# Attention and a gated Mish MLP on one core: the PSUM layout of the scores, the order of the engines and the spread of 1/den are changed together

## The chip, the core and the metric

The kernel runs on one core of one Trainium2 chip. The metric is the device time in microseconds (us) of one launch. PE is the engine of the matmuls, ACT the engine of the activations (here the exponential), DVE the vector engine, SP the engine that issues most DMAs. PSUM, which the matmuls write into, is used as eight banks of 128 x 512 f32. The granted clock is the share of its full clock that PE was allowed.

## The reference

```python
a = softmax(q k^T * Dh**-0.5) v @ wo       # S = 2048, D = 640, H = 32 heads, Dh = 20
h = x @ w1 + b1                            # F = 1536
b = (h * tanh(softplus(h))) @ w2           # Mish MLP
g = sigmoid((x * gate_w).sum(-1))
return g * a + (1 - g) * b                 # bf16 inputs
```

## The kernel before

The work of the attention is 2048 **blocks**: 128 keys x 512 queries of one head. Four heads share the row strips of PE, and 64 blocks make a **group** (one chunk of 512 queries, four heads), of which there are 32. Each block needs a score matmul, an exponential and a PV matmul. Four blocks (the four heads) form one **quad** of PV, whose matmuls run side by side in the column strips of PE.

The exponentials are the largest job. ACT does most of them, 2 or 3 blocks in one instruction. 232 of the 2048 blocks go to DVE. It turns the scores into bits of an exponential with a first pass out of PSUM (`dA`, one per block, 0.69 us), and then works on pairs of blocks in a chain of five operations that leaves three bf16 terms (`dN`, `dA`, `dB`) whose sum is the exponential. PV of such a block therefore takes three rounds where others take one.

PSUM before: score tiles alternate between 3 and 2 banks (5 banks), one bank is the accumulator of PV (`acc`), and 2 banks serve the projections (x transposed, k, q, v, the MLP and `wo`) and also the scores of the DVE blocks, which are computed up to 20 blocks ahead.

```python
WIDTHS = (3, 2); LEAD = 20
banks = [psum.tile([P, QC], F32, tag=f"bank{i}", name=f"bank{i}") for i in range(2)]
epool = ctx.enter_context(tc.tile_pool(name="epool", bufs=3))

def emit_D(n):                              # scores of a DVE block: a projection bank
    d = banks[ubank[0] ^ 1]
    bank_free[ubank[0] ^ 1] = now[0] + 1
    scores(d[:, :], blocks[n])
    nc.vector.tensor_scalar(out=A[:, i, :], in0=d[:, :], scalar1=exp_c, scalar2=0.0,
                            op0=ALU.add, op1=ALU.max)            # first pass
    # [cut: every second block queues the chain of five operations]

for t, ns in enumerate(tiles):              # one turn per score tile
    w = WIDTHS[t % 2]
    E = epool.tile([P, w, QC], BF16, tag=f"E{t % 2}", bufs=3 - t % 2, name="E")
    nc.scalar.activation(E[:, 0:nw, :], sp.pop(t)[:, 0:nw, :], ACT.Exp, scale=escale)
    emit_S(t + 2)                           # the next scores into the same tile
    # [cut: emit_D at most every second turn; two operations of the DVE chain]
    used += pv_quads(min(tiles[t + 1][0], n_end), t)             # PV of blocks before tile t+1
    credit -= pump(min(credit, max(room, 300.0)), 1)             # projections, fixed budget
```

At the end of a group, `acc` is copied to `accS`, its row of denominators goes through four small DMAs to `den`, DVE takes the reciprocal `rec`, four more small DMAs of 2 KB bring it to one row per strip, a shuffle on DVE spreads it over the strip, and a multiply writes `oT`.

The softmax here doesn't subtract the row's maximum and nothing guards it: scores larger than these inputs give would overflow.

## Time and profile before

| kernel before | |
|---|---|
| median of the runs | 997.37 us (993.48 to 1002.19, 4 runs) |
| profiled run: span, mean granted clock | 995.7 us, 0.902 |
| ACT busy / PE busy / DVE busy | 876.3 / 874.1 / 647.8 us |
| ACT idle from 25 us to the last exponential | 21 us in slices at full clock, 58 us in slices that touch a lowered clock |

The last row comes from cutting the span into slices of 5 us. 705 us of slices had a granted clock of 1.00, and 240 us had less.

The page of the kernel before: the span, busy time by engine (share of the span, number of instructions), busy tenths of PE, ACT and the granted clock in 40 slices, and the group of the exponentials (count, then busy us and mean ns, then idle time of ACT just before them and what ended most of it).

```profile
span 995.7 us, 15399 instructions
PE 874.1 (88%) x6181; PEld 270.5 (27%) x6250; DVE 647.8 (65%) x1269; ACT 876.3 (88%) x751; POOL 19.0 (2%) x36
...
PEclk7999999998699789999967999996999996995877
...
L755 ACT ACTIVATE E<-Sp 128x1536 bf16<-128x1536 f32 x727 | 841.0, 1261 | 80.5 <-PE Sp L576 65.3
```

Here `Sp` is a score tile in PSUM, `E` the buffer in SBUF that an exponential writes, and `<-PE Sp` says that a PE instruction on `Sp` ended the wait. PE and ACT are nearly level. ACT waits mostly for scores, 65 of its 80 us. The groups by form of the same kernel give one exponential of each width:

```profile
L755 ACT ACTIVATE E<-Sp 128x1536 bf16<-128x1536 f32 x363 | 534.8, 1473 | 54.8 <-PE Sp L576 48.6 <-PE bank_73 L576 2.4 <-PE bank_74 L576 0.7
L755 ACT ACTIVATE E<-Sp 128x1024 bf16<-128x1024 f32 x363 | 381.0, 1050 | 25.6 <-PE Sp L576 16.7 <-PE bank_73 L576 6.0 <-PE bank_74 L576 1.7
```

The widths alternate, so every pair of neighbours is of two forms. The two forms add to 915.8 us and cover 841.0, so neighbours overlap by 75 us in all, 0.10 us per exponential. The Trainium skill, "ScalarE: Activation LUTs", section "What ACT_TABLE_LOAD costs", gives about 93 ns for this overlap; the trace has somewhat more here.

The windows of the kernel before (length, then busy time and count of PE, PEld, DVE, ACT, POOL, then granted clock, DMA share, GB/s). The first is a stretch with many projections. The next three stand around a Mish step, in which ACT ran something other than exponentials and PE stood 7.71 us for a score tile. The last two belong to a later low stretch.

```profile
core 0: us, PE busy (x) PEld busy (x) DVE busy (x) ACT busy (x) POOL busy (x), PEclk, DMA share, GB/s
25.00:200.00 175.00, 162.42 (x1383) 62.37 (x1403) 100.07 (x232) 161.66 (x142) 3.12 (x6) 0.99 0.02 4
...
325.00:330.00 5.00, 2.29 (x14) 0.63 (x13) 3.88 (x8) 4.97 (x4) 0.00 (x0) 0.91 0.00 0
330.00:335.00 5.00, 0.01 (x1) 0.01 (x1) 0.00 (x0) 4.97 (x5) 0.00 (x0) 0.50 0.00 0
335.00:340.00 5.00, 5.00 (x25) 1.15 (x25) 0.79 (x2) 3.90 (x4) 0.00 (x0) 0.56 0.00 0
...
900.00:905.00 5.00, 5.00 (x23) 0.90 (x22) 0.69 (x1) 2.69 (x3) 0.00 (x0) 0.50 0.00 0
905.00:910.00 5.00, 5.00 (x23) 1.16 (x22) 3.54 (x7) 4.00 (x4) 0.00 (x0) 0.50 0.00 0
```

At half clock PE is full (5.00 of 5) and ACT is not. So two things limit this kernel: ACT at full clock, PE at half clock.

### The profile page before, as it was taken

Reading aid. Unit: us, or ns where it says so; the run is one execution under the profiler, and the core shown is the slowest. Engines: PE = TensorE matmul, PEld = TensorE weight load, DVE = VectorE, ACT = ScalarE, POOL = GpSimd, SP = SyncE. Lnnn points to the kernel's source line nnn. Section 1 sums busy time; section 2 is a strip of 40 time slices with the busy share of each in tenths; the row PEclk is TensorE's granted clock in tenths of the full one; section 3 lists DMA queues with packets and bytes.
Section 4 is the critical chain, followed back from the end, with each engine's and each line's share of the span. In section 5 each row is a group of like instructions: output and inputs, shape, how many; then the busy total and the mean of one; then the engine's idle time right before and its main releaser. Section 6 shows DMA issues by size and latency. Waiting matters only on the chain.

```text
span 995.7 us, 15399 instructions
## 1 busy us (share of the span) xinstructions
PE 874.1 (88%) x6181; PEld 270.5 (27%) x6250; DVE 647.8 (65%) x1269; ACT 876.3 (88%) x751; POOL 19.0 (2%) x36
## 2 busy tenths in 40 slices
PE   5999998888898688999979998997998969889894
PEld 2433332222222122332212322221332212221221
DVE  2455646677676567777846876774777764774665
ACT  3899999899898989999988999989999997996881
POOL 6000000000000000000000000000000000000000
PEclk7999999998699789999967999996999996995877
DMA  7100000004000000000000000000000000000000
GB/s 231 16 2 2 1 2 1 1 2 140 21 2 1 1 1 2 15 8 9 2 1 1 2 15 8 8 1 1 2 1 2 1 1 8 9 15 1 2 1 27
DMA packets 22216, 14.18 MB, mean 14 GB/s; under 512 B 15968, under 2 KB 20192, under 8 KB 22144
## 3 DMA queue, kind: packets, MB, share of 16 engines
q1 hardware_dynamic: 20512, 12.16, 4.0%
q0 software_dynamic: 320, 0.82, 0.4%
q8 instruction: 49, 0.80, 0.3%
q10 hardware_dynamic: 1312, 0.20, 0.1%
q14 instruction: 23, 0.19, 0.1%
HBM read 10.04 MB, written 2.62 MB: 13 GB/s over the span
## 4 chain that ended last, share of the span: by engine, by line
PE 45%; ACT 29%; DVE 14%; issue 7%; DMA 3%; SPq 2%; DVEq 0%; ACTq 0%; another core or an unknown queue 0%
ACT E L755 26%; PE Sp L576 13%; PE acc L649 13%; PE bank_74 L366 3%; PE bank_73 L366 3%; DVE dA L600 3%; PE bank_73 L231 2%; PE bank_74 L231 2%; ACT hst L354 2%; PE bank_74 L332 2%; PE bank_74 L576 1%; PE bank_73 L332 1%; DVE dm L626 1%; DVE rrow L685 1%; DMA rrow<-rec 1%
## 5 line engine op out<-in xcount | busy, mean ns | idle before, releaser
L755 ACT ACTIVATE E<-Sp 128x1536 bf16<-128x1536 f32 x727 | 841.0, 1261 | 80.5 <-PE Sp L576 65.3
L576 PE MATMUL Sp<-qT,kT 32*128 32x512 bf16 x1816 | 310.7, 408 | 61.8 <-ACT E L755 52.3
L649 PE MATMUL acc<-E,VA 128*32 128x512 bf16 x1816 | 214.0, 416 | 6.3 <-DVE accS L666 6.0
L576 PEld LDWEIGHTS <-kT 32*128 32x128 bf16 x2048 | 82.4, 92 | 270.1 <-issue 250.0
L600 DVE TENSOR_SCALAR dA<-bank_73 128x512 int16<-128x512 f32 x116 | 79.7, 687 | 104.6 <-PE bank_73 L576 101.0
L600 DVE TENSOR_SCALAR dA<-bank_74 128x512 int16<-128x512 f32 x116 | 79.1, 682 | 72.2 <-PE bank_74 L576 71.7
L649 PEld LDWEIGHTS <-VA 128*32 128x32 bf16 x2512 | 69.4, 96 | 188.1 <-issue 174.9
L626 DVE TENSOR_TENSOR dm<-dm 128x1024 f16<-128x1024 f16 x116 | 79.9, 689 | 2.6
L628 DVE TENSOR_TENSOR dB<-dA,dm 128x1024 bf16<-128x1024 bf16 x116 | 79.4, 684 | 0.0
L576 PE MATMUL bank_74<-qT,kT 32*128 32x512 bf16 x116 | 46.2, 398 | 13.0 <-DVE hst L340 6.4
L623 DVE TENSOR_SCALAR dm<-dm 128x1024 f16<-128x1024 bf16 x116 | 49.9, 430 | 4.0
L619 DVE TENSOR_SCALAR dm<-dA 128x1024 int16<-128x1024 int16 x116 | 49.6, 427 | 4.0
L649 PE MATMUL acc<-dN,VA 128*32 128x512 bf16 x232 | 50.0, 428 | 0.1
L649 PE MATMUL acc<-dA,VA 128*32 128x512 bf16 x232 | 49.4, 423 | 0.0
L576 PE MATMUL bank_73<-qT,kT 32*128 32x512 bf16 x116 | 47.9, 413 | 1.6 <-DVE kT L240 1.6
L649 PE MATMUL acc<-dB,VA 128*32 128x512 bf16 x232 | 49.2, 421 | 0.0
L627 DVE TENSOR_SCALAR dN<-dA 128x1024 int16<-128x1024 int16 x116 | 48.8, 420 | 0.0
L366 PE MATMUL bank_74<-w_sb,hst 128*128 128x320 bf16 x204 | 47.6, 325 | 1.0 <-DVE dA L600 0.6
L366 PEld LDWEIGHTS <-hst 128*128 128x128 bf16 x384 | 28.4, 99 | 61.0 <-issue 56.5
L366 PE MATMUL bank_73<-w_sb,hst 128*128 128x320 bf16 x180 | 41.0, 324 | 1.9 <-DVE dA L600 1.7
L332 PE MATMUL bank_74<-xT,w_sb 128*128 128x512 bf16 x115 | 38.6, 391 | 4.1 <-DVE dA L600 3.7
L666 DVE COPY accS<-acc 128x512 f32<-128x512 f32 x31 | 21.4, 690 | 24.6 <-PE acc L649 24.6
(102 smaller groups left out, 610.4 us busy)
## 6 DMA issues: line engine op xcount, KB each, us to landing
w_sb<-in_B_w_dram SPq DMA_DIRECT2D x2, 1920.0 KB, 11.1
x_sb<-in_A_x_dram SPq DMA_DIRECT2D x4, 640.0 KB, 7.7
out_dram<-ot SPq DMA_DIRECT2D x16, 160.0 KB, 1.8
den<-accS SPq DMA_DIRECT2D x124, 2.0 KB, 1.7
rrow<-rec SPq DMA_DIRECT2D x124, 2.0 KB, 1.7
W_sb<-in_A_wqkv_dram SPq DMA_DIRECT2D x1, 1600.0 KB, 15.1
W_sb<-in_A_wqkv_dram SPq DMA_DIRECT2D x1, 800.0 KB, 8.2
wo_sb<-in_A_wo_dram POOLq DMA_DIRECT2D x4, 200.0 KB, 6.6
```

Of the source, the lines that this page charges most:

```text
L231: nc.tensor.matmul(cell["t"][:, :], lhsT=lhs(kt), rhs=xT[:, kt, c * QC : (c + 1) * QC], start=(kt == 0), stop=(kt == KT - 1),)
L332: nc.tensor.matmul(cell["t"][:, :], lhsT=lw["w1"][:, kt, ft * P : (ft + 1) * P], rhs=xT[:, kt, c * QC : (c + 1) * QC], start=(kt == 0), st ...
L366: nc.tensor.matmul(cell["t"][:, :], lhsT=lhs(k, jj), rhs=rhs(k)[:, cols], start=(k == k0), stop=(k == k1 - 1),)
L576: nc.tensor.matmul(dst, lhsT=kT[R * r : R * (r + 1), p, j * P : (j + 1) * P], rhs=qTs[c, p][R * r : R * (r + 1), :], start=True, stop=True ...
L600: nc.vector.tensor_scalar(out=A[:, i, :], in0=d[:, :], scalar1=exp_c, scalar2=0.0, op0=ALU.add, op1=ALU.max)
L619: lambda: ts(out=m, in0=A, scalar1=0x7F, scalar2=0x3F80, op0=ALU.bitwise_and, op1=ALU.bitwise_or,),
L623: lambda: ts(out=t, in0=mf, scalar1=exp_k, scalar2=exp_k * EXP_M, op0=ALU.mult, op1=ALU.add),
L626: lambda: tt(out=t, in0=t, in1=t, op=ALU.mult),
L627: lambda: ts(out=N, in0=A, scalar1=0x7F80, scalar2=None, op0=ALU.bitwise_and),
L628: lambda: (tt(out=B, in0=Ab, in1=t, op=ALU.mult), done_()),
L649: nc.tensor.matmul(acc[R * r : R * (r + 1), :], lhsT=VA[:, j, p, (DH + 1) * r : (DH + 1) * r + R], rhs=es[r][k], start=(j == 0 and k == 0) ...
L755: nc.scalar.activation(E[:, 0:nw, :], sp.pop(t)[:, 0:nw, :], ACT.Exp, scale=escale)
```

## The change

The intent: put each DVE block into a score tile, so that the scores of three blocks always run together in the row strips of PE; give both score tiles three banks, and pay for that with one of the two projection banks; decide the order of PE's instructions by a virtual clock that models when each engine will be ready; and replace the four DMAs and the shuffle of 1/den by a DMA to a scratch in DRAM and one DMA back that spreads each row over its 32 partitions.

The diff also changes smaller things: estimated costs of projections, the order of some units of the MLP, 10 instead of 12 buffers for `oT`, and 236 instead of 232 DVE blocks. The diff, cut to its core:

```diff
-    WIDTHS = (3, 2)
-    LEAD = 20
+    BPT = 3
+    DPOS0 = (2, 3, 10, 11)
+    DPOS = (1, 2, 6, 7, 11, 12)
-    banks = [psum.tile([P, QC], F32, tag=f"bank{i}", name=f"bank{i}") for i in range(2)]
+    bank = psum.tile([P, QC], F32, tag="bank")
-    epool = ctx.enter_context(tc.tile_pool(name="epool", bufs=3))
+    epool = ctx.enter_context(tc.tile_pool(name="epool", bufs=5))
[cut]
+    def on_dve(t):
+        g = tiles[t][-1] // 64
+        return g > 0 and t + 2 < len(tiles) and t % 16 in (DPOS0 if g < 5 else DPOS)
[cut]
     def ahead(n):
-        return tile_at[max(0, n - LEAD)] - 4
+        return tile_at[n] - 5
[cut]
     def emit_S(t):
-        w = WIDTHS[t % 2]
-        sp[t] = psum.tile([P, w, QC], F32, tag=f"S{t % 2}", name="Sp")
-        for i, n in enumerate(tiles[t]):
+        ns = tiles[t]
+        sp[t] = psum.tile([P, BPT, QC], F32, tag=f"S{t % 2}", name="Sp")
+        for i, n in enumerate(ns):
             scores(sp[t][:, i, :], blocks[n])
+        V["pe"] = max(V["pe"], s_ready(t) - 0.1) + pe_cost(0.213, "S")
+        s_done[t] = V["pe"] + 0.23
+        if on_dve(t):
+            dve_score(ns[-1], sp[t][:, BPT - 1, :], t)     # first pass from the third bank
[cut: normalise]
+            scr = scrp.tile([4, QC], F32, tag="scr", name="scr")
+            nc.sync.dma_start(scr.rearrange("r (i n) -> (r i) n", n=ND), rec)
+            v = scr[:, :]
+            nc.sync.dma_start(rr[:, :], bass.AP(v.tensor, v.offset, [[QC, 4], [0, R], [1, QC]]))
-            nc.vector.stream_shuffle(out=rr, in_=rr, mask=[0] * R)
-        later[t + 4] = part1
-        later[t + 8] = part2
+        later.append((V["dve"] + 3.0, 0.25, part1))
+        later.append((V["dve"] + 9.0, 0.69, part2))        # the multiply
[cut: the turn of tile t]
-        E = epool.tile([P, w, QC], BF16, tag=f"E{t % 2}", bufs=3 - t % 2, name="E")
+        na = len(ns) - on_dve(t)
+        E = epool.tile([P, BPT, QC], BF16, tag="E", name="E")
+        nc.scalar.activation(E[:, 0:na, :], sp.pop(t)[:, 0:na, :], ACT.Exp, scale=escale)
+        begin = max(V["act"], s_done[t])
+        V["act"] = begin + 0.05 + 0.427 * na
+        credit = min(credit + min(rate(t), 2600.0), 2600.0)
+        late_by = 0.6 if credit > 2300.0 else 0.05
+        while True:
+            q, u = next_quad(), next_step() if credit > 0 else None
+            behind = 3 * t - 4 * quad[0] >= 10
+            [cut: the PV quad q or the projection step u, whichever fits before ACT needs S]
+        while 3 * (t + 1) - 4 * quad[0] > 12 and 4 * quad[0] + 4 <= 3 * (t + 1):
+            [cut: finish the DVE chain if it must]
+            pv_quad()                                      # forced
```

## The prediction

> **What bounds it now.** The page: PE and ACT each busy 88% of 995.7 us, DVE 65%. In slices of 5 us between 25 and 975 us (windows view): 720 us at full granted clock, where ACT idles only 23 us; 230 us touch a lowered clock, where ACT idles 58 us. At full clock the exponentials (841 us, 727 instructions) are the limit, PE close behind; at half clock PE is, with about three exponentials in 5 us against 5.5. The first exponential starts at 19.3 us, the last ends about 21 us before the end.
>
> The Trainium skill ("TensorE: Matmul & The Clock Gate", "HAM oscillation") says that PE gaps above about 3.4 us drop the clock to half. The trace agrees for Mish: PE stood 7.71 us from 327 us on, and 330 to 335 us ran at 0.50. Other low stretches begin after PE stood behind DVE: 1.57 us at 185 us, 0.88 us at 894 us, both before a DVE-score matmul.
>
> **What changes, costed.**
> - ACT: 683 exponentials (447 of three banks, 236 of two). By form they last 1.473 and 1.050 us and overlap by about 0.10. Estimate: 447 x 1.473 + 236 x 1.050 - 683 x 0.10 = about 836 us, 5 saved, on the path.
> - PE scores: 232 separate DVE-score matmuls vanish into the three-wide tile, whose row strips run together. About 145 followed a run of three or five blocks and cost about 0.22 us each (timeline); 44 fewer tiles at 0.21. About 40 us less.
> - PE switches between scores, PV and projections cost about 0.1 us (timeline). In the instruction order the runs fall from 1840 to 1468: about 37 us less.
> - PE PV: 236 DVE blocks sit in about 190 quads instead of 116, each with two extra rounds of 0.213: about 32 us more.
> - PE net about -45 us of 874: hidden at full clock, mostly visible at half clock.
> - DVE: 31 shuffles (22 us) go. The scores' first pass (0.69 us) now frees a bank of the score tile, but has more than one exponential's time for it. One projection bank costs PE about 1 us between units, filled with scores and PV by the virtual clock.
> - 1/den: two DMAs with a DRAM round trip replace four of 1.7 us landing. The multiply may hold DVE up to 1 us, 31 times; mostly hidden.
>
> **Sum.** 19 start + 21 end + about 866 ACT after its start (836 + Mish and tables) + full-clock idle 15 to 20 + low-clock idle 25 to 35 (58 before: PE has 5% less work there, and the waits behind separate DVE scores go). About 950 us. The four Mish gaps stay.
>
> Predicted **950 us**, 8 in 10 within **925 to 980**. Faster by over 2%: 0.87; within 2%: 0.10; slower: 0.03.
>
> **What would show it right.** 683 exponentials, about 835 us busy, idle before them 40 to 55 us; PV busy up by about 30 us; mean granted clock 0.91 to 0.94 with fewer low stretches outside Mish; small waits of scores on DVE's first pass (under 10 us) and of DVE on the rr DMA (under 20 us).
>
> **What would make it wrong.** The clock gate: if the single bank or the wait on DVE's first pass makes new PE holes, low stretches multiply and the gain halves. If the virtual clock drifts from the chip, PE stands at the head of its queue for the bank. If low stretches vanish altogether, below 930.

## The result and the profile after

The changed kernel took **1170.22 us** (median of 4 runs, 1167.6 to 1181.72) against 997.37 us. The ratio is **1.1753 [1.1657, 1.1849]**: slower by 17.5%. A ratio is the mean time of one kernel's fast runs over that of the other's fast runs of the same rounds, so it is not quite the ratio of the two medians. Executions over 1.5% slower than the fastest of the same kernel are left out of the means.

The page after, with the same lines. The profiled run is the slowest of the four (1181.72 us; the others lie 9 to 14 us below), so its idle times are a little high.

```profile
span 1179.9 us, 15520 instructions
PE 885.9 (75%) x6190; PEld 302.9 (26%) x6258; DVE 637.7 (54%) x1221; ACT 882.2 (75%) x707; POOL 18.5 (2%) x35
...
PEclk6899986898779899798887799988879879787987
...
L781 ACT ACTIVATE E<-Sp 128x1536 bf16<-128x1536 f32 (+1 forms) x683 | 846.9, 1305 | 251.6 <-PE acc L675 142.8
```

No engine works much longer than before: ACT 882 us instead of 876, PE 886 instead of 874, DVE 10 less. ACT stands idle instead, 252 us before its exponentials against 80. Summed over slices of 5 us from 25 us to the last exponential, ACT idles 256 us (121 at full clock, 135 at a lowered one) against 80 (21 and 58). That is 176 us more, and the span grew by 184. So the question is what ACT waited for. The groups by form after:

```profile
L781 ACT ACTIVATE E<-Sp 128x1536 bf16<-128x1536 f32 x446 | 619.0, 1455 | 122.6 <-PE acc L675 86.6 <-PE Sp L576 35.9
L781 ACT ACTIVATE E<-Sp 128x1024 bf16<-128x1024 f32 x237 | 238.7, 1022 | 129.0 <-DVE dA L610 65.1 <-PE acc L675 56.2 <-DVE dN L644 3.9
```

The main releaser is new: `PE acc`, that is, a PV matmul. An exponential does not need PV for its input. It needs it for its output: it writes a buffer `E` that an older PV must have read. The second releaser is `DVE dA`, the first pass of the DVE block, and it stands only in the two-bank form, the tiles whose third bank is a DVE block. Neighbours are now often of the same form, and a form's busy time leaves their overlap out, so the overlap is taken from counts and means: 446 x 1455 ns + 237 x 1022 ns is 891 us, and they cover 846.9. The overlap of neighbours has shrunk from 75 us to 44, because fewer exponentials follow each other directly (428 overlapping pairs against 555).

The waits after (who waited for whom, us in total, times, longest us). Before, the row of `PE Sp` waiting for ACT had 52.3 us in 77 waits.

```profile
PE Sp L576 <- ACT E L781: 202.1, 331, 5.8
ACT E L781 <- PE acc L675: 142.8, 116, 4.1
...
ACT E L781 <- DVE dA L610: 65.1, 90, 2.1
...
ACT E L781 <- PE Sp L576: 35.9, 25, 6.9
...
DVE oT L715 <- DMA rr<-scr: 33.1, 14, 4.9
```

PE waits for ACT and ACT waits for PE: the two take turns. A piece of the timeline after shows how (start, duration, engine, instruction, count; in brackets the idle time before it and its releaser):

```profile
714.75 2.79 ACT L781 ACTIVATE E<-Sp 128x1536 bf16<-128x1536 f32 x2 [0.88 <-PE acc L675]
715.86 0.58 SPq L708 DMA_DIRECT2D rr<-scr  x1
716.25 0.39 PE L576 MATMUL Sp<-qT,kT 32*128 32x512 bf16 x3 [0.47 <-ACT E L781]
...
717.59 0.39 PE L576 MATMUL Sp<-qT,kT 32*128 32x512 bf16 x3 [0.43 <-ACT E L781]
717.92 0.40 PE L675 MATMUL acc<-E,VA 128*32 128x512 bf16 x3
...
718.41 2.79 ACT L781 ACTIVATE E<-Sp 128x1536 bf16<-128x1536 f32 x2 [0.86 <-PE acc L675]
...
720.79 0.69 DVE L715 TENSOR_TENSOR oT<-accS,rr 128x512 bf16<-128x512 f32 x1 [4.87 <-DMA rr<-scr]
721.40 0.68 DVE L610 TENSOR_SCALAR dA<-Sp 128x512 int16<-128x512 f32 x1
```

Read it from 717.54, where two exponentials end (714.75 + 2.79). Only now may PE write the next score tile, at 717.59. The PV that reads the old `E` stands behind it in PE's order, from 717.92 to 718.32, and only then does the next exponential start, at 718.41. Its own scores had been ready since 716.6. ACT lost 0.86 us although it had input.

Counts from the instruction order of the built program support this. For the exponential of tile t, the last PV that reads its buffer stands behind the scores of tile t+1 in 105 of 678 cases, behind the scores of tile t in another 237, and before them in the rest. (The PV of a DVE block reads `dN`, `dA` and `dB` and no `E`, so it does not count.) The 105 are those that cannot run back to back with the exponential before. 105 x 0.87 us (the mean of the two gaps above) would be 91 us of the 142.8; the trace has 116 waits of 1.23 us in the mean, so this count gives the larger part of the wait and not all of it. The kernel before also had five buffers (three wide, two narrow), but there the PV never stands behind the scores of tile t. The reason for the late PVs is the lag: when PE comes to the scores of tile t+2, the newest tile that PV has read is t-1 or t-2 before (but for the first two tiles), and as far back as t-4 or t-5 in 246 of 683 turns after, with a ring of 5 buffers.

The last two lines of the timeline show a third thing. DVE stood for 4.87 us before the multiply `oT`, which needs the spread 1/den; a first pass `dA` stood behind it in DVE's order and started only at 721.40. The DMA of 256 KB had been issued at 715.86.

The windows after, with the stretch that answers to the first one shown of before, and three us of the same DMA:

```profile
25.00:200.00 175.00, 134.57 (x1141) 55.90 (x1159) 79.24 (x188) 125.38 (x98) 2.60 (x5) 0.89 0.04 10
...
717.00:720.00 3.00, 1.65 (x15) 0.68 (x13) 0.00 (x0) 2.14 (x3) 0.00 (x0) 1.00 0.24 81
```

In the first 175 us after 25, ACT worked 125.38 us instead of 161.66. And while the spreading DMA ran, the mean busy share of the 16 DMA engines was 0.24, which is four of them.

**Theories at this point.**
- R (ring): the ring of five `E` buffers is too short for the lag of PV; it costs the 143 us that ACT waits for `PE acc`.
- D (first pass): the two-bank exponentials wait for DVE's first pass of the same tile; once R is gone this wait stays or grows.
- N (1/den): the multiply stands in DVE's queue for the DMA and delays the first pass.
- C (clock): the granted clock fell (0.902 to 0.862 in the profiled runs) through some new PE holes, and the slow PE makes the waits.
- B (bank): one projection bank starves the stretch with many projections.

The expectations below use other letters: their A is R, their B is D, and their C is N.

### The profile page after: what moved, and what is told of

It reads as the page before. It is cut to its first block, busy times and chain, and to the rows that moved or that the text cites. A ratio compares the mean times of both kernels' runs of the same rounds, so it can differ in the third digit from the quotient of the medians.

```text
span 1179.9 us, 15520 instructions
## 1 busy us (share of the span) xinstructions
PE 885.9 (75%) x6190; PEld 302.9 (26%) x6258; DVE 637.7 (54%) x1221; ACT 882.2 (75%) x707; POOL 18.5 (2%) x35
## 4 chain that ended last, share of the span: by engine, by line
PE 37%; ACT 30%; issue 13%; DVE 12%; DMA 8%; ACTq 0%; another core or an unknown queue 0%; SPq 0%; DVEq 0%
ACT E L781 27%; PE Sp L576 12%; PE acc L675 11%; DMA rr<-scr 5%; PE bank L360 4%; DVE dA L610 4%; PE bank L225 4%; PE bank L326 3%; DMA scr<-rec 2%; ACT hst L348 1%; PE bank L267 1%; DVE kT L234 1%; DVE hst L334 1%; DVE oT L715 1%; DMA W_100<-in_A_wqkv_dram 1%
## 5 line engine op out<-in xcount | busy, mean ns | idle before, releaser
L781 ACT ACTIVATE E<-Sp 128x1536 bf16<-128x1536 f32 (+1 forms) x683 | 846.9, 1305 | 251.6 <-PE acc L675 142.8
L610 DVE TENSOR_SCALAR dA<-Sp 128x512 int16<-128x512 f32 x236 | 161.8, 688 | 222.6 <-PE Sp L576 221.4
L675 PE MATMUL acc<-dB,VA 128*32 128x512 bf16 x236 | 82.1, 427 | 10.4 <-DVE dB L645 10.3
L360 PE MATMUL bank<-w_sb,hst 128*128 128x320 bf16 x384 | 80.1, 325 | 7.9 <-ACT hst L348 6.2
L675 PE MATMUL acc<-dN,VA 128*32 128x512 bf16 x236 | 83.5, 433 | 2.6 <-DVE dN L644 2.6
L675 PE MATMUL acc<-dA,VA 128*32 128x512 bf16 x236 | 82.7, 429 | 0.0
L326 PE MATMUL bank<-xT,w_sb 128*128 128x512 bf16 x215 | 74.7, 433 | 9.8 <-DVE hst L334 7.0
L334 DVE TENSOR_SCALAR hst<-bank,b1f 128x512 f32<-128x512 f32 x48 | 35.9, 749 | 43.5 <-PE bank L326 43.2
L360 PE MATMUL bank<-wo_sb,oT 128*128 128x320 bf16 x248 | 53.0, 329 | 5.0 <-DVE T_c L386 3.2
L225 PE MATMUL bank<-xT,wqp 128*128 128x512 bf16 x136 | 43.9, 411 | 5.3 <-DVE kT L234 2.8
L715 DVE TENSOR_TENSOR oT<-accS,rr 128x512 bf16<-128x512 f32 x31 | 21.3, 686 | 33.2 <-DMA rr<-scr 33.1
```

The source lines that it names most:

```text
L225: nc.tensor.matmul(cell["t"][:, :], lhsT=lhs(kt), rhs=xT[:, kt, c * QC : (c + 1) * QC], start=(kt == 0), stop=(kt == KT - 1),)
L326: nc.tensor.matmul(cell["t"][:, :], lhsT=lw["w1"][:, kt, ft * P : (ft + 1) * P], rhs=xT[:, kt, c * QC : (c + 1) * QC], start=(kt == 0), st ...
L360: nc.tensor.matmul(cell["t"][:, :], lhsT=lhs(k, jj), rhs=rhs(k)[:, cols], start=(k == k0), stop=(k == k1 - 1),)
L610: nc.vector.tensor_scalar(out=A[:, i, :], in0=ps, scalar1=exp_c, scalar2=0.0, op0=ALU.add, op1=ALU.max)
L675: nc.tensor.matmul(acc[R * r : R * (r + 1), :], lhsT=VA[:, j, p, (DH + 1) * r : (DH + 1) * r + R], rhs=es[r][k], start=(j == 0 and k == 0) ...
L781: nc.scalar.activation(E[:, 0:na, :], sp.pop(t)[:, 0:na, :], ACT.Exp, scale=escale)
```

## The experiments

18 kernels ran; all gave correct results. "Before" beside a median is the median of the kernel before on the same chip in the same set. These medians include its slow runs, so differences to the kernel before are taken from the ratios, which leave them out. Experiments of different sets are compared by ratio. In sets 1, 4 and 6 two to four of the seven runs of the kernel before were slow, and the record's verdict there (at a threshold of 2%) is "unclear"; their intervals are printed.

### Set 1: ring and 1/den, alone and together

More buffers than five do not fit beside the other tiles (with eight, the buffers of the MLP needed 59.03 KB per partition where 50.3 were left, and the kernel did not build), so the input of Mish is first kept in bf16 to make room. That edit alone is the control `hst_bf16`.

```diff
# hst_bf16, against the changed kernel
-            hsts[c] = late.tile([P, FT, QC], F32, tag="hst", name="hst")
+            hsts[c] = late.tile([P, FT, QC], BF16, tag="hst", name="hst")   # and its views
# ring9, against hst_bf16
-    epool = ctx.enter_context(tc.tile_pool(name="epool", bufs=5))
+    epool = ctx.enter_context(tc.tile_pool(name="epool", bufs=9))
# old_den, against the changed kernel: four small DMAs and the shuffle of before
-            nc.sync.dma_start(rr[:, :], bass.AP(v.tensor, v.offset, [[QC, 4], [0, R], [1, QC]]))
+            for r in range(4):
+                nc.sync.dma_start(rr[R * r : R * r + 1, :].rearrange(...), rec[R * r : R * (r + 1), :])
+            nc.vector.stream_shuffle(out=rr, in_=rr, mask=[0] * R)
# ring9_old_den: ring9 and old_den together
```

> Control for the next run: the changed kernel with only the Mish input stored in bf16 instead of fp32, which frees 12 KB of a partition and changes no order. All theories: 1160 to 1185 us, within 1% of the changed kernel; the exponentials' wait for PV (143 us there) stays above 120 us.

Measured: 1177.92 us (before 998.81), ratio 1.1905 [1.1741, 1.207]. ACT waits for `PE acc` 146.5 us in 122 waits, for `DVE dA` 62.5. The interval overlaps that of the changed kernel ([1.1657, 1.1849]): the bf16 input alone changes nothing that shows, so the next run can be compared with it. The wait of `hst_bf16`, which the next run is to remove:

```profile
ACT E L776 <- PE acc L670: 146.5, 122, 3.5
```

> The same with 9 instead of 5 buffers for the exponentials' output; the order of instructions on every engine is the same. Theory A (the ring of 5 makes an exponential wait for a PV that stands behind a later score tile in PE's order): the wait for PV falls from 143 us to under 15 us, and the time falls to 1000 to 1060 us. Rival B (exponentials wait because ACT and DVE are kept from reading one score tile at once): the wait for DVE's first pass stays at 60 us or grows and the time stays above 1100 us. Rival C (the multiply's wait for the 1/den DMA holds DVE and all behind it): above 1120 us.

Measured: 1074.43 us, ratio 1.0894 [1.0789, 1.0999]. The waits of `ring9`:

```profile
ACT E L776 <- DVE dA L605: 97.1, 134, 3.3
...
ACT E L776 <- PE Sp L571: 50.1, 48, 6.9
...
DVE oT L710 <- DMA rr<-scr: 41.1, 21, 4.5
```

The wait for `PE acc` is gone altogether, and 103 us with it. The instruction order is the same in both kernels, so this is the ring and nothing else. R is shown. The time lies above the 1000 to 1060 us that were expected of R alone and below the 1100 us of its rival D, which is a second cause. The idle time of ACT fell from 252 to 151 us by the slices. But the wait for DVE's first pass grew from 62.5 to 97.1 us. The timeline of `ring9` shows one such wait:

```profile
598.72 1.47 ACT L776 ACTIVATE E<-Sp 128x1536 bf16<-128x1536 f32 x1
...
599.20 0.39 PE L571 MATMUL Sp<-qT,kT 32*128 32x512 bf16 x3
599.31 0.69 DVE L236 TENSOR_SCALAR qT<-bank 128x512 bf16<-128x512 f32 x1 [0.73 <-PE bank L225]
599.91 0.68 DVE L605 TENSOR_SCALAR dA<-Sp 128x512 int16<-128x512 f32 x1
...
600.69 1.02 ACT L776 ACTIVATE E<-Sp 128x1024 bf16<-128x1024 f32 x1 [0.51 <-DVE dA L605]
```

The scores are there at 599.59, ACT is free at 600.19, and the two-bank exponential starts at 600.69, 0.10 us after `dA` ended. DVE had first to empty the projection bank (`qT`). The exponential reads banks 0 and 1 and DVE reads bank 2, so neither needs the other's result.

> The changed kernel with 1/den spread as before (four small DMAs and a shuffle in place of the DRAM round trip), ring of 5. Theory A: the 33 us of DVE's wait for the DMA go, the exponentials' wait for PV stays above 110 us, 1130 to 1160 us. Rival C: 1000 to 1070 us, and the wait for PV falls with it to under 60 us.

Measured: 1154.87 us, ratio 1.1694 [1.1496, 1.1892], 23 us below `hst_bf16`. ACT waits for `PE acc` still 134.6 us.

> Both: 9 buffers and the old 1/den. Theory A with C as a second, smaller cost: 15 to 40 us below the run with 9 buffers alone, 970 to 1030 us, at the level of the kernel before or a little below. If B carries most, above 1080 us.

Measured: 1043.56 us, ratio 1.0566 [1.0482, 1.0651], 31 us below `ring9`. ACT waits for `DVE dA` 75.8 us in 130 waits. The median lies a little above the range that was expected, because that wait stayed. So N is real, 23 us with the short ring and 31 with the long one, and part of its gain shows in the wait for the first pass (97.1 to 75.8). The clock came back with the waits: 0.871, 0.918, 0.936 in the profiled runs of `hst_bf16`, `ring9` and `ring9_old_den`, without any edit aimed at it. So C is not needed as a first cause: the clock follows the waits. That it adds to them while they last is likely, since PE is full at half clock, but no run shows how much.

### Set 2: why ACT waits for DVE's first pass

Four runs on the base of `ring9_old_den`. One rival said that the DVE blocks stand in neighbouring tiles (positions 1, 2 and 6, 7 and so on), so that the second pass queues behind the first on DVE. The other said that the wait is in the program: two instructions that read different banks of one PSUM tile are ordered one after the other. In the built program 235 of the 237 two-bank exponentials carry a wait on DVE's semaphore, and no three-bank one does; in the program of `split_two` below, no exponential does.

```diff
# spread: no neighbours
-    DPOS0 = (2, 3, 10, 11)
-    DPOS = (1, 2, 6, 7, 11, 12)
+    DPOS0 = (2, 5, 10, 13)
+    DPOS = (1, 4, 6, 9, 11, 14)
# exp_first: the first pass is issued after the exponential of the tile, not before
+        if on_dve(t):
+            s_done[t] = e_done[t]
+            dve_score(ns[-1], sp[t][:, BPT - 1, :], t)
# split_one: a three-bank exponential is issued as 2 + 1 banks; still one tile (control)
+        nc.scalar.activation(E[:, 0:n2, :], st[:, 0:n2, :], ACT.Exp, scale=escale)
+        if na == 3:
+            nc.scalar.activation(E[:, 2:3, :], st[:, 2:3, :], ACT.Exp, scale=escale)
# split_two: the same exponentials, but the third bank is a PSUM tile of its own
+        s2 = psum.tile([P, 2, QC], F32, tag=f"S{t % 2}", name="Sp")
+        x1 = psum.tile([P, 1, QC], F32, tag=f"X{t % 2}", name="Sx")
```

> 9 buffers, old 1/den, and the DVE blocks never in two neighbouring tiles (tiles 1, 4, 6, 9, 11, 14 of 16 in place of 1, 2, 6, 7, 11, 12). Theory B, refined: after a two-bank exponential (about 0.95 us) the next score tile's DVE pass can't be done in time (score 0.4 + pass 0.69 + two hand-overs, about 1.25 us), so the second of two neighbours makes ACT wait. Then ACT's wait for the pass falls from 76 us to under 35 us and the time from 1043 to 1000 to 1025 us, although PV gets some 70 rounds more. If the wait comes from the DVE queue being behind with other work, it stays above 60 us and the time within 1035 to 1060 us.

Measured: 1103.3 us (before 990.76), ratio 1.1095 [1.1002, 1.1189]. Slower, not faster, and outside both ranges that were expected. ACT waits for `DVE dA` as long as ever (76.2 us in 78 waits), and PE now waits for DVE's terms (`dN` 46.6 us in 34 waits, `dB` 15.1). So the wait is not cured by keeping the blocks apart; but this run brought waits of its own, so a part of the neighbours in it is not excluded.

> 9 buffers, old 1/den, and the exponential of a tile issued before its DVE pass, so that the pass waits for ACT and no exponential waits for the pass. If keeping ACT and DVE apart in one tile is a cost in either order, ACT's wait moves to the scores of two tiles later (freed by the pass 0.9 us after the exponential): wait for the pass 0, wait for scores up from 44 to 80 to 120 us, time 1030 to 1080 us. If only the present order costs, below 1000 us.

Measured: 1070.79 us, ratio 1.0765 [1.068, 1.0849]. The wait of ACT for the pass is gone, but DVE now waits for ACT (126.9 us in 132 waits), PE for DVE (94.7 us), and ACT for PE's scores (147.6 us in 194 waits, more than the 80 to 120 expected). The order was turned round; it was not taken away.

> Control for the next: 9 buffers, old 1/den, each three-bank exponential issued as two banks and one bank. 446 instructions more at about 0.1 to 0.2 us: ACT 920 to 960 us busy, time 1070 to 1110 us, the wait for the pass 40 to 80 us.

> The same exponentials, but the third bank is a tile of its own, so no exponential of a DVE tile waits for the DVE pass. Theory B: the wait for the pass falls to about 0 and the time to 30 to 70 us below the control. If the wait was only a sign of PE being late, the same idle time turns up as a wait for scores, and the two lie within 10 us.

Measured: `split_one` 1066.25 us, ratio 1.0736 [1.0674, 1.0799]; `split_two` 995.09 us, ratio 1.0028 [0.9979, 1.0076]. The control lies just below its expected range (ACT was busy 902.2 us, not 920 to 960), and the gain of 71 us just above its own. The two kernels issue the same exponentials in the same order. By form, first `split_one`, then `split_two`:

```profile
L779 ACT ACTIVATE E<-Sp 128x1024 bf16<-128x1024 f32 x683 | 700.5, 1042 | 123.8 <-DVE dA L607 79.1 <-PE Sp L573 42.1 <-ACT E L781 0.4
L781 ACT ACTIVATE E<-Sp 128x512 bf16<-128x512 f32 x446 | 281.7, 632 | 0.0
```

```profile
L783 ACT ACTIVATE E<-Sp 128x1024 bf16<-128x1024 f32 x683 | 716.9, 1102 | 59.3 <-PE Sx L575 45.8 <-PE Sp L575 11.0
L785 ACT ACTIVATE E<-Sx 128x512 bf16<-128x512 f32 x446 | 298.7, 670 | 1.2 <-PE Sx L575 1.2
```

71 us go with the wait for `dA`. D is shown: the wait belongs to the tile, not to the data, and the result stays correct without it. The Trainium skill, "PSUM — Partial Sum Buffer", section "PSUM bank collisions raise a hardware error", says that accesses of two engines to different banks run clean together; `split_two` agrees, with a correct result and no wait of ACT for the pass at all. The granted clock rose to 0.949.

### Set 3: was it really the wait, and what else

```diff
# split_two_xfirst, against split_two: the one-bank exponential is issued first
-        nc.scalar.activation(E[:, 0:n2, :], s2[:, 0:n2, :], ACT.Exp, scale=escale)
         if na == 3:
             nc.scalar.activation(E[:, 2:3, :], x1[:, :, :], ACT.Exp, scale=escale)
+        nc.scalar.activation(E[:, 0:n2, :], s2[:, 0:n2, :], ACT.Exp, scale=escale)
# split_two_ring5, against split_two
-    epool = ctx.enter_context(tc.tile_pool(name="epool", bufs=9))
+    epool = ctx.enter_context(tc.tile_pool(name="epool", bufs=5))
# spread_lag, against spread: PV is forced later
-            behind = 3 * t - 4 * quad[0] >= 10
+            behind = 3 * t - 4 * quad[0] >= 18
-        while 3 * (t + 1) - 4 * quad[0] > 12 and 4 * quad[0] + 4 <= 3 * (t + 1):
+        while 3 * (t + 1) - 4 * quad[0] > 20 and 4 * quad[0] + 4 <= 3 * (t + 1):
# alt, against ring9_old_den: even tiles are one tile of three banks with one exponential,
# odd tiles are 2 + 1; DVE blocks in odd tiles only; PV forced later (16, 14)
-    DPOS = (1, 2, 6, 7, 11, 12)
+    DPOS = (1, 3, 7, 9, 11, 13)
+        if t % 2 == 0:
+            s3 = psum.tile([P, BPT, QC], F32, tag="S0", name="Sp")
+        else:
+            s2 = psum.tile([P, 2, QC], F32, tag="S1", name="Sp")
+            x1 = psum.tile([P, 1, QC], F32, tag="X1", name="Sx")
# [cut: the positions of the first groups, the exponentials of the odd tiles as in split_two]
```

> As the run with the third bank in a tile of its own (995 us), but the one-bank exponential is issued ahead of the two-bank one, so that the two-bank tile comes free last and PE can't refill it early. If the gain of 71 us came from no longer keeping ACT behind the DVE pass: 990 to 1015 us. If it came from PE's earlier refill of two of the three banks: 1040 us or more.

Measured: 1003.95 us (before 996.67), ratio 1.0083 [1.0043, 1.0123]. In `split_two` PE may refill the first two banks as soon as the first exponential is done, which `split_one` does not allow. If that early refill had made the 71 us, turning the order round would have given most of it back. It gave back about half a per cent (1.0083 against 1.0028, in two sets), as was expected if the wait is the cause.

> As the run with the third bank in a tile of its own, with 5 buffers for the exponentials' output in place of 9 and the same order. If the ring is a cost of its own: wait for PV 90 to 150 us, time 1070 to 1110 us. If the ring's wait was only there because the exponentials stood behind the DVE pass: below 1020 us.

Measured: 1129.54 us, ratio 1.1354 [1.1277, 1.1432]; ACT waits for `PE acc` again:

```profile
ACT E L783 <- PE acc L676: 141.4, 136, 3.5
```

Without the wait for the pass the short ring costs 13% by itself, more than was expected. R and D are separate causes, and they overlap: with nine buffers `split_two` stands at 1.0028 against 1.0566 of its base, with five at 1.1354 against 1.1694 of `old_den`.

> The run with DVE blocks in no two neighbouring tiles (1103 us), with the rule that forces a PV at 12 blocks of lag moved to 20 (and 10 to 18). That run's PE stood 62 us behind the DVE chain of PVs so forced. If the forcing spoiled it: PE's wait for dN and dB under 15 us, ACT's wait for the pass under 45 us, 1000 to 1040 us. If spreading itself is bad: above 1070 us.

Measured: 1055.25 us, ratio 1.0606 [1.0562, 1.065]. Later forcing took away most of PE's waits for `dN` and `dB` (3.1 us are left for `dB`) and nearly all that `spread` had lost against its base `ring9_old_den` (1.1095 to 1.0606, the base 1.0566), but brought no gain over it: ACT waits for `DVE dA` 90.7 us, and DVE's pass now waits for `PE acc` 42.7 us in 35 waits, because late PVs hold DVE's own two `dA` buffers. The expectation missed.

> A version meant to beat both: 9 buffers, old 1/den, even tiles of three banks in one exponential, odd tiles of two banks and one, DVE blocks in odd tiles only (1, 3, 7, 9, 11, 13 of 16), forced PV at 16 blocks. ACT about 880 us busy (796 exponentials and others), no wait for the DVE pass, wait for PV under 10 us: 955 to 985 us. If ACT's extra idle time is PE's, it stays at 990 us or more.

Measured: 990.35 us, ratio 0.9953 [0.9908, 0.9999]. Splitting only the odd tiles brings ACT's busy time down from 891.0 us (`split_two`) to 871.8. The time missed the 955 to 985 us that were expected and stands at the 990 us of the other reading, that the rest of ACT's idle time is PE's.

### Set 4: the projection stretch, and the multiply

`alt` still idles in the stretch from 25 to 200 us: ACT works 142.86 us of 175, against 161.66 before. Two parts of the change could do that apart from the single bank: the deadlines of the projections, and the ceiling of the credit that each turn may spend on them.

```diff
# alt_lead, against alt: deadlines as before
-        return tile_at[n] - 5
+        return tile_at[max(0, n - 20)] - 4
# alt_cap, against alt
-        credit = min(credit + min(rate(t), 2600.0), 2600.0)
-        late_by = 0.6 if credit > 2300.0 else 0.05
+        credit = min(credit + min(rate(t), 3600.0), 3600.0)
+        late_by = 0.6 if credit > 3300.0 else 0.05
# alt_lead_cap: both
# ring9_late_mul, against ring9: the DRAM way stays, DVE reaches the multiply later
-        later.append((V["dve"] + 9.0, 0.69, part2))
+        later.append((V["dve"] + 15.0, 0.69, part2))
```

> The alt version (990 us) with the deadlines of the K and Q projections moved 20 blocks ahead, as the kernel before had them. In alt ACT idles 32 us between 25 and 200 us, where before idled 13 us, and scores there stand behind a projection that was just made. If the shorter lead does it: ACT's idle time in that stretch falls to under 20 us, 970 to 982 us. If the one projection bank does it: no change within 5 us.

> Alt with the ceiling of projection work per tile raised from 2600 to 3600 columns, deadlines as in alt. If the ceiling holds early projections back: ACT idle in 25 to 200 us under 22 us, 972 to 984 us. If the bank or the deadlines do it: within 5 us of alt.

> Both. If they add up: 960 to 978 us. If the one projection bank is the limit in that stretch: 983 us or more.

Measured (before 994.88): 990.27 us, ratio 1.002 [0.9957, 1.0082]; 985.79 us, 0.9976 [0.9912, 1.0041]; 981.79 us, 0.993 [0.9857, 1.0003]. ACT worked 141.98, 143.76 and 145.04 us of the 175. Within this set the ceiling is worth 8.5 us on top of the deadlines, and the deadlines 4.0 us on top of the ceiling; the deadlines alone show no gain. `alt` itself ran in another set (ratio 0.9953), so what the two bring together lies between 2 us by the ratios and 9 us by the medians, within the noise of the ratios. Neither was the cause as expected: ACT still idles 30 to 33 us in that stretch.

> The changed kernel with 9 buffers and its own 1/den by DRAM (1074 us), but the multiply by 1/den is put in DVE's order 15 instead of 9 us after the copy. If the DRAM way costs because DVE reaches the multiply before the spread has landed: DVE's wait for it falls from 41 us to under 5 us, and the time to 1040 to 1052 us, the level of the old 1/den. If the DMA traffic itself costs: 1065 us or more.

Measured: 1027.08 us, ratio 1.0426 [1.0316, 1.0536]; DVE waits for the DMA once, 2.9 us. This is better than `ring9` (1.0894), better than the 1040 to 1052 us expected, and no worse than the old way (`ring9_old_den`, 1.0566, whose interval overlaps). So the spread by DMA is not bad; what was bad is that DVE was sent to the multiply before the data could be there.

### Set 5: the best version of the parts

```diff
# alt_all, against alt_lead_cap: 1/den through DRAM, with the late multiply
+            nc.sync.dma_start(rr[:, :], bass.AP(v.tensor, v.offset, [[QC, 4], [0, R], [1, QC]]))
+        later.append((V["dve"] + 15.0, 0.69, part2))
```

> The alt version with earlier deadlines and the higher ceiling (982 us), with the DRAM 1/den back in and its multiply 15 us after the copy, which was 16 us better than the old 1/den in the run with 9 buffers. If that gain carries over: 960 to 972 us, faster than before by over 2%, DVE's wait for the spread under 5 us. If in that run it came only from slack around the DVE pass, which alt no longer waits for: 976 to 986 us.

Measured in 5 rounds: 982.64 us (before 990.34), ratio **0.9932 [0.9895, 0.9968]**: 0.7% faster than the kernel before, the best of all runs that was measured this closely. The hope for 960 to 972 us failed and the other reading, 976 to 986 us, came true: the spread by DMA with the late multiply brought nothing here that `alt_lead_cap` (0.993) had not. Where ACT does not wait for DVE's pass, how 1/den is spread does not show in the time. The waits and a window of `alt_all`:

```profile
PE Sp L571 <- ACT E L786: 54.9, 103, 5.6
ACT E L786 <- PE Sp L571: 29.4, 37, 7.3
ACT E L788 <- PE Sx L571: 26.6, 22, 5.4
...
DVE oT L718 <- DMA rr<-scr: 2.4, 1, 2.4
```

```profile
25.00:200.00 175.00, 150.22 (x1294) 59.44 (x1293) 90.95 (x211) 144.34 (x145) 3.13 (x6) 0.98 0.04 10
200.00:950.00 750.00, 658.88 (x4824) 213.23 (x4821) 523.98 (x959) 714.96 (x658) 0.00 (x0) 0.96 0.06 19
```

### Set 6: one projection bank in the kernel before

```diff
# before_one_bank, against the kernel before: projections stay in one bank, DVE scores in the other
     def next_bank():
-        ubank[0] ^= 1
         return banks[ubank[0]][:, :]
     def ready(key):
-        if now[0] and bank_free[ubank[0] ^ 1] > now[0]:
+        if now[0] and bank_free[ubank[0]] > now[0]:
```

> The kernel before with all projections in one of its two banks and the separate DVE scores always in the other. The versions that shed the three waits still let ACT idle about 30 us between 25 and 200 us, where the projections are, against 13 us in the kernel before. If one projection bank is the reason: ACT's idle time there rises by 10 us or more over before's 13, total 1005 to 1040 us. If one bank is harmless: idle there within 4 us of before's, total within 1% of before.

Measured: 1049.9 us (before 992.16), ratio 1.0623 [1.0523, 1.0723]. The windows of `before_one_bank`:

```profile
25.00:200.00 175.00, 145.74 (x963) 53.85 (x978) 60.94 (x148) 109.71 (x94) 2.08 (x4) 0.71 0.02 3
200.00:970.00 770.00, 660.82 (x4729) 205.44 (x4780) 529.03 (x1005) 707.69 (x605) 1.26 (x2) 0.93 0.03 9
```

All of the loss falls into the stretch with many projections: there ACT worked 109.71 us instead of 161.66, and from 200 us on it worked 707.69 of 770, where the kernel before worked 703.61. So one bank, with this scheduler, can cost there. The clock fell too in this stretch (0.71 against 0.99), so part of the 52 us may be the clock's, and the scheduler is the old one, with fixed budgets. Its rule `bank_free` also has a side effect here: after the first group it lets a projection start two turns after the last one ended, where two banks in turn let it start on the next. So the bank and this rule are not told apart, and the size does not carry over to the changed kernel.

### The runs in one table

ACT idle is summed over slices of 5 us from 25 us to the last exponential, in the profiled runs. The last slice reaches past that exponential and can add up to 5 us.

| kernel | us | ratio to before | ACT idle, full / lowered clock |
|---|---|---|---|
| before | 997.37 | 1 | 21 / 58 |
| changed | 1170.22 | 1.1753 | 121 / 135 |
| `hst_bf16` (control) | 1177.92 | 1.1905 | 120 / 132 |
| `ring9` | 1074.43 | 1.0894 | 95 / 56 |
| `ring9_old_den` | 1043.56 | 1.0566 | 91 / 37 |
| `split_one` (control) | 1066.25 | 1.0736 | 87 / 40 |
| `split_two` | 995.09 | 1.0028 | 46 / 17 |
| `alt` | 990.35 | 0.9953 | 47 / 30 |
| `alt_lead_cap` | 981.79 | 0.993 | 45 / 19 |
| `alt_all` | 982.64 | 0.9932 | 46 / 22 |

## Why the prediction was wrong

The direction and the size were wrong: 950 us with 0.87 for faster, and 1170 us measured. Point by point:

1. **A term that the sum did not have: the ring of `E`.** The prediction's sum is "19 start + 21 end + about 866 ACT after its start + full-clock idle 15 to 20 + low-clock idle 25 to 35". Nothing in it asks where an exponential may write. The diff showed five buffers, and the built order showed the PV that frees a buffer behind the scores of the next tile in 105 cases; the two together give the wait. The prediction expected 40 to 55 us of idle time before the exponentials, and 251.6 came. ACT waited 142.8 us for PV. Nine buffers, with the same order, took the whole wait away and 103 us with it (`hst_bf16` to `ring9`); in `split_two_ring5` the ring alone costs 13%. The virtual clock has the same hole: its start of an exponential is `max(V["act"], s_done[t])`, engine and scores, without the buffer.

2. **"The scores' first pass (0.69 us) now frees a bank of the score tile, but has more than one exponential's time for it."** The prediction looked for the wait at the scores ("small waits of scores on DVE's first pass (under 10 us)"). Those were indeed small: no such wait of PE is in the list after. The wait sat with ACT: 65.1 us, 97.1 with nine buffers, because the exponential of the same tile was ordered behind the pass. A tile of its own for the third bank was worth 71 us (`split_one` to `split_two`).

3. **"The multiply may hold DVE up to 1 us, 31 times; mostly hidden."** It held DVE up to 4.9 us, 33.1 us in 14 waits. The cost was about 23 us with the short ring (`old_den`) and 31 to 47 us with the long one (`ring9` to `ring9_old_den` and to `ring9_late_mul`, in two sets, so the second is 4.7% of the time of before by the ratios). It was visible, at least in part, for the reason of point 2: the pass behind the multiply held ACT, whose wait for it fell from 97.1 us to 75.8 and 67.1. In `alt_all`, where no pass holds ACT, the late multiply adds nothing. That few engines carry the transfer could have been read off: the Trainium skill, "DMA: Bandwidth & Descriptors", section "Why a DMA increments its semaphore by 16 and not by 1", says that a DMA uses the largest number of engines, up to 16, that divides the outermost dimension of both sides. The source here starts with a dimension of 4. The trace agrees: a mean share of 0.24 of 16 engines, at 81 GB/s. A pattern that uses all 16 was not run.

4. **"One projection bank costs PE about 1 us between units, filled with scores and PV by the virtual clock."** Of this, full-clock idle of 15 to 20 us was expected; `alt_all`, free of the first three causes, has 46. From 25 to 200 us ACT idles 30.7 us there (175 - 144.34) against 13.3 before. `before_one_bank` shows that a single bank, with the old scheduler, can cost in just this stretch; deadlines and ceiling explain 9 us at most. How the rest is shared between the bank and the scheduler stays open.

5. **ACT's busy time.** 835 us expected, 846.9 measured, and the number of exponentials (683) was right. The mistake is the term "683 x 0.10" of overlap: it needs exponentials that follow each other, and 44 us of overlap came instead of 68. The single exponentials were a little shorter than expected (891 us in all against 906), which hid part of it.

6. **What was right.** PV busy was to go up by about 30 us: PE was busy with PV 303.9 us in `alt_all` (310.1 in the changed kernel, at a lower clock) against 273.6. The low-clock idle was to fall to 25 to 35 us from 58: 22 in `alt_all`, once the new waits were gone. The mean clock was to be 0.91 to 0.94: 0.952 there. PE was to be busy about 45 us less, from 874: 836.1 there, though 885.9 in the changed kernel at its lower clock. So the parts that the sum did hold were roughly sized. But with the waits gone the measured gain is 0.7%, not 4.7%, and most of the difference is the idle time at full clock of point 4: 46 us where 15 to 20 were expected, out of 32 us between 950 and 982.64.

The clock had been named as the main risk, "if the single bank or the wait on DVE's first pass makes new PE holes, low stretches multiply". Low stretches did multiply (445 us of slices below full clock against 240), but each run that took a wait away brought the clock back, so it was a follower. More than half of ACT's 256 us of idle time lies in slices with a lowered clock; how much of that the clock itself made was not shown.

## What to carry to other kernels

When a change moves the order of a consumer, count for every producer which consumer frees its output buffer and where that stands in the order: a ring must be longer than the largest lag, or two engines take turns. Two engines that read different banks should read different tiles, because the order that a program keeps may go by the tile and not by the bank. A schedule from a model is only as good as its list of waits; when the chip is slower than the model, look first for a wait that the model does not have.

## What the Trainium skill lacked or had wrong

- "TensorE: Matmul & The Clock Gate", section "What's actually happening", has the clock return to full after about 3.4 us of sustained work. In the kernel before, PE was busy 5.00 of 5 us in every slice from 900 to 920 us and the granted clock stayed at 0.50 through all four; the same from 510 to 525 us. The nearest that the page has is a caveat in its section "Seeing it yourself": a clock seen stuck for over 50 us, but at a quarter and not at half. (Busy time of PE has modelled ends, so short holes inside may be hidden.)
- The same page, section "HAM oscillation — how this bites in real kernels", gives gaps above about 3.4 us as what lowers the clock. The trace agrees for the gap of 7.71 us (0.50 from 330 to 335 us). But the low stretch at 895 us begins after two gaps of 0.24 and 0.88 us, with PE busy 3.88 of 5 us. The page's section "A second HAM failure mode: psum-queue depth-cycling" does say that frequent short gaps can make the clock go up and down; what it lacks is how much idle time in how long a stretch is enough, and no run here settles that.
- "PSUM — Partial Sum Buffer" says that different banks run clean together, which `split_two` agrees with. No page that I read says that reads of different banks of one tile by two engines come out ordered in the program; that cost 65 to 97 us of ACT's time here, and 71 us of the total.
- "DMA: Bandwidth & Descriptors" was right, and not used: its rule of the outermost dimension gives 4 engines, and the trace shows a share of 0.24. No run shows what 16 would have brought.
